# Moving layer-norm and division steps between chunks of a fused attention and feed-forward kernel, and summing its last three chunks tile by tile

## The chip, the core and the metric

The kernel runs on one core of a Trainium2 chip. The metric is device time in microseconds (us). The core has five engines with a queue each: TensorE (PE in the profile; its weight loads are PEld), VectorE (DVE), ScalarE (ACT), GpSimd (POOL) and SyncE (SP), which here only issues transfers (DMAs). Every queue runs in order: an instruction that waits holds up all behind it on its engine. [...]

## What is computed

One transformer block with adaptive layer norm over 2048 tokens of width 512. Cut to what matters:

```python
x = x + ga * attention(layernorm(x) * (1 + ca) + sa)      # 32 heads of 16
h = layernorm(x) * (1 + cb) + sb
x = x + gb * (gelu(h @ w1 + b1) @ w2 + b2)                # 512 -> 1792 -> 512
```

The attention output is divided by the sum of the softmax and multiplied by `wo`. Inputs and outputs are float32.

## The kernel before

Tokens are handled in four blocks of 512 (`NB`, `TB`), which the change's description calls first to fourth; in the code they are 0 to 3. A product of two float32 operands is made from three matmuls on a high and a low part of each operand, so each operand that meets TensorE is first split: a cast gives the high part, a subtraction the low part.

The kernel has three stages: projections, attention, feed-forward. The change touches the last one alone, the loop at lines 984 to 996. It takes 56 steps (`NI`), one for each block and each 128 columns of the 1792 hidden ones; step i is chunk i % 14 of block i // 14. A step does this, in the order in which each engine's queue receives it:

- `load_f(i + 4)`, line 717: SyncE issues the two weight loads of the step four ahead (w1r, w2r, 256 KB each).
- `split_f(i + 2)`, line 724: the weights of the step two ahead are split. VectorE casts w1h (line 728) and w2h (line 730); GpSimd subtracts for w1l (line 729) and w2l (line 731).
- `ffn1(i)`, line 895: 12 matmuls (line 300) into one PSUM bank of the ring `sc`; ScalarE makes g, the gelu (line 903), and ghi (line 906); VectorE subtracts for glo (line 907).
- `ffn2([i - 1])`, line 912: 12 matmuls (line 924) add the step before to four accumulators, one for each tile of 128 tokens: ghi with w2h, ghi with w2l, glo with w2h. So TensorE asks for glo of step i at the third matmul of `ffn2([i])`, which stands in step i + 1. With the last chunk of a block in its list, `ffn2` also ends the block: y = accumulator * gb on VectorE (line 929, four times, three buffers), then x2 + y (line 933) on GpSimd, in the last block on VectorE, and a store from SyncE (line 934). For blocks 0 to 2 that falls into steps 14, 28 and 42.
- the functions that `plan` lists for the step.

The plan carries what the later blocks need. `o_load` (line 758) fetches the attention output of a block as o_b; `o_den` (line 751) inverts the softmax sums and stores them. `o_norm` (line 766) is the division, for each of four parts k: a load of the inverse sums, rb (line 775, SyncE, 256 KB), then on VectorE a multiplication (line 778), a cast (line 779) and a subtraction (line 780). `o_proj` (line 790) is 12 matmuls with `wo` and one addition on VectorE (line 802). `ln2` (line 806) is the layer norm: statistics of four tiles (line 236), a factor rs that GpSimd raises to a power (line 241), and for each tile a pair of VectorE operations, xn_b (line 813) and x2 + b2 (line 814). `ln2_t` (line 819) transposes on TensorE (line 257), lets ScalarE scale into a tile h (line 262) and VectorE split it (lines 263, 264).

`put_ln2` (line 956) spreads a layer norm around a step n that it is given: statistics of three tiles in step n - 1, the fourth and rs in n, two pairs in n + 1, two pairs in n + 2, transposes in n + 4 and n + 5. Nothing is reordered: the four lists are written out by hand in lines 971 to 983.

The buffers that the steps meet: rb and h share three buffers (tag `h32` of `epool`), ghi and glo have three each (lines 904, 905), the split weights four.

Of the kernel before, what the change touches and what calls it, by code (L numbers as in the profile page):

```python
# [22 lines left out]
NF = FF // P  # L23
# [29 lines left out]
def block_kernel(ctx: ExitStack, tc: tile.TileContext, x, wqkv, wo, w1, b1, w2, b2, c, w_mod, out):  # L53
# [4 lines left out]
    def pool(name, bufs=1, **kw):  # L58
        cm = tc.tile_pool(name=name, bufs=bufs, **kw)
        return cm, cm.__enter__()  # L60

    def close(cm):
        cm.__exit__(None, None, None)
# [15 lines left out]
    def bank_mx():  # L79
        return ring("mx")  # L80

    def bank():
        return ring("sc")

    def bank_pv():
        return ring("pv")
# [568 lines left out]
    epool = ctx.enter_context(tc.tile_pool(name="epool", bufs=1, side="right"))  # L655
# [60 lines left out]
    def load_f(i):  # L716
        f = i % NF
        a = fpool.tile([P, KC, P], F32, tag="w1r", name="w1r", bufs=3)
        b = fpool.tile([P, D], F32, tag="w2r", name="w2r", bufs=3)
        sy.dma_start(a, w1[:, f * P : (f + 1) * P].rearrange("(k p) n -> p k n", p=P))  # L720
        sy.dma_start(b, w2[f * P : (f + 1) * P, :])
        raw1[i] = a, b

    def split_f(i):
        a, b = raw1.pop(i)
        ahi, alo = [fpool.tile([P, KC, P], FR, tag=n, name=n, bufs=4) for n in ("w1h", "w1l")]
        bhi, blo = [fpool.tile([P, D], FR, tag=n, name=n, bufs=4) for n in ("w2h", "w2l")]
        ve.tensor_copy(ahi, a)  # L728
        gp.tensor_tensor(alo, a, ahi.bitcast(F32), op=ALU.subtract)  # L729
        ve.tensor_copy(bhi, b)  # L730
        gp.tensor_tensor(blo, b, bhi.bitcast(F32), op=ALU.subtract)  # L731
        wf[i] = ahi, alo, bhi, blo
# [5 lines left out]
    def parts8(pl):  # L738
        if pl is epool:
            t = kts[len(p8) % 2 - 1]  # L740
            p8.append([t[:, i].rearrange("p (k t) -> p k t", k=KC) for i in range(2)])
            return p8[-1]
        return [pl.tile([P, KC, TB], FR, tag=n, name=n, bufs=1) for n in ("h2hi", "h2lo")]
# [7 lines left out]
    def o_den(qb):  # L751
        dn = dns[qb]
        ve.reciprocal(dn, dn)
        sy.dma_start(rden_d[qb].rearrange("h (a f) -> (h a) f", f=P), dn)
# [3 lines left out]
    def o_load(qb):  # L758
        obs[qb] = o_b
        sy.dma_start(obs[qb], o_d[qb].rearrange("(k p) t -> p k t", p=P))  # L760
        if qb < 3:
            oo[qb] = parts8(epool)
        else:
            oo[qb] = [fpool.tile([P, KC, TB], FR, name=f"o3{i}", bufs=1) for i in range(2)]

    def o_norm(qb, k):

        ob = obs[qb]
        ohi, olo = oo[qb]
        eng = ve if qb > 1 else gp  # L770

        def load():
            rbs[qb, k] = epool.tile([P, TB], F32, tag="h32", name="rb", bufs=3)
            r = rden_d[qb][k * 8 : (k + 1) * 8]
            sy.dma_start(rbs[qb, k], bass.AP(tensor=r.tensor, offset=r.offset, ap=[[TB, 8], [0, DH], [1, TB]]))

        return [load,
                lambda: eng.tensor_tensor(ob[:, k], ob[:, k], rbs[qb, k], op=ALU.mult),
                lambda: eng.tensor_copy(ohi[:, k], ob[:, k]),
                lambda: eng.tensor_tensor(olo[:, k], ob[:, k], ohi[:, k].bitcast(F32), op=ALU.subtract)]  # L780
# [3 lines left out]
    def load_x2(qb, x2t):  # L784
        x2[qb] = x2t
        for i in range(4):
            r0 = qb * TB + i * P
            sy.dma_start(x2t[i], x[r0 : r0 + P, :])

    def o_proj(qb, t):  # L790

        ohi, olo = oo[qb]
        ps = []
        sl = slice(t * P, (t + 1) * P)
        terms = [(p[:, i, sl], w[:, i]) for i in range(KC) for p, w in ((ohi, wo_hi), (ohi, wo_lo), (olo, wo_hi))]

        def mm(i):
            if i == 0:
                ps.append(bank() if qb else bank_mx())
            te.matmul(ps[0], *terms[i], start=i == 0, stop=i == len(terms) - 1)  # L800
            if i == len(terms) - 1:
                ve.tensor_tensor(x2[qb][t], ps[0], x2[qb][t], op=ALU.add)

        return [lambda i=i: mm(i) for i in range(len(terms))]

    def ln2(qb):

        mv = small.tile([P, 4, 2], F32, tag="mv", name="mv")
        rs = small.tile([P, 4], F32, tag="rs", name="rs")
        xns[qb] = [xn_b[:, t] for t in range(4)]  # L810

        def rows(t):
            ve.tensor_scalar(xns[qb][t], x2[qb][t], mv[:, t, 0:1], rs[:, t : t + 1], op0=ALU.subtract, op1=ALU.mult)
            ve.tensor_tensor(x2[qb][t], x2[qb][t], b2_b, op=ALU.add)

        return ([lambda t=t: ln_stat(mv, t, x2[qb][t]) for t in range(4)] + [lambda: ln_factor(mv, rs)]
                + [lambda t=t: rows(t) for t in range(4)])

    def ln2_t(qb, pl):
        hi, lo = parts8(pl)  # L820
        tr, evac = transposed(xns.pop(qb), hi, lo, 1, epool, lambda fc: bank(), (ve, ve))
        h2[qb] = hi, lo
        return [lambda fc=fc: evac(fc, tr(fc)) for fc in range(KC)]
# [67 lines left out]
    fcm, fpool = pool("fpool", bufs=2)  # L891
# [20 lines left out]
    def ffn2(fs):  # L912
        qb = fs[0] // NF
        if fs[0] % NF == 0:
            acc[qb] = [bank_mx(), bank_mx(), bank_mx(), bank_pv()]
        ops = []
        for i in fs:
            ghi, glo = gt.pop(i)
            _, _, bhi, blo = wf.pop(i)
            ops += [(i % NF, n, p, q) for n, (p, q) in enumerate(((ghi, bhi), (ghi, blo), (glo, bhi)))]  # L920
        for t in range(4):
            sl = slice(t * P, (t + 1) * P)
            for f, n, p, q in ops:
                te.matmul(acc[qb][t], p[:, sl], q, start=f == 0 and n == 0, stop=f == NF - 1 and n == 2)  # L924
            if ops[-1][0] == NF - 1 and t:
                ts = (0, 1) if t == 1 else (t,)
                ys = [fpool.tile([P, D], F32, tag="y", name="y", bufs=3) for _ in ts]
                for i, y in zip(ts, ys):
                    ve.tensor_tensor(y, acc[qb][i], gb_b, op=ALU.mult)
                for i, y in zip(ts, ys):  # L930
                    r0 = qb * TB + i * P
                    eng = ve if qb == NB - 1 else gp
                    eng.tensor_tensor(x2[qb][i], x2[qb][i], y, op=ALU.add)
                    sy.dma_start(out[r0 : r0 + P, :], x2[qb][i])

    NI = NB * NF
# [16 lines left out]
    def put(qb, f, *fs):  # L953
        plan.setdefault((qb, f), []).extend(fs)

    def put_ln2(qb, at, pl):

        i0 = at[0] * NF + at[1]

        def step(key, make, i):  # L960
            if i == 0:
                steps[key] = make()
            steps[key][i]()

        for i in range(9):
            n = i0 + (-1 if i < 3 else 0 if i < 5 else 1 if i < 7 else 2)
            put(*divmod(n, NF), lambda i=i: step((qb, "l"), lambda: ln2(qb), i))
        for i in range(4):
            put(*divmod(i0 + 4 + i // 2, NF), lambda i=i: step((qb, "t"), lambda: ln2_t(qb, pl), i))

    put(0, 0, lambda: o_load(2), lambda: o_den0(3))
    put(0, 3, lambda: o_den(3))
    put(0, 7, lambda: o_load(3))
    for t in range(4):
        for i, d in enumerate((0, 1, 1, 2)):
            put(0, 1 + t + d, lambda t=t, i=i: o_norm(2, t)[i]())
            put(0, 8 + t + d, lambda t=t, i=i: o_norm(3, t)[i]())
        put(0, 8 + t, lambda t=t: [f() for f in o_proj(2, t)])
        put(1, 5 + t, lambda t=t: [f() for f in o_proj(3, t)])
    put(1, 1, lambda: load_x2(3, x2[0]))  # L980
    put_ln2(1, (0, 1), fpool)
    put_ln2(2, (0, 13), epool)
    put_ln2(3, (1, 11), fpool)
    for i in range(NI):
        qb, f = divmod(i, NF)
        if i + 4 < NI:
            load_f(i + 4)
        if i + 2 < NI:
            split_f(i + 2)
        ffn1(i)  # L990
        if i and i < NI - 2:
            ffn2([i - 1])
        for fn in plan.get((qb, f), []):
            fn()
    ffn2([NI - 3])
    ffn2([NI - 2, NI - 1])
    close(fcm)
    close(kcm)

# [25 lines left out]
```

## Time and profile before

| what | us |
|---|---|
| median of 3 runs (lowest to highest) | 1766.52 (1766.45 to 1767.83) |
| the profiled execution's own time | 1765.35 |
| its span, first to last instruction | 1763.6 |
| the 56 steps, from the first `ffn1` matmul to the last matmul's end | 1420.4 to 1758.6 |

The span is 1.75 us shorter than the profiled execution's own time, and that is 1.17 us under the median. In the timelines a row gives start, busy time, engine, line, operation, output and inputs, and in brackets the engine's idle time before it with what ended it. Where two operations follow each other without idle time, the distance of their starts is what counts: the busy time of a row reaches a little into the next row.

### The profile page before, as it was taken

How to read it: one execution, taken by the hardware profiler on the slowest of the kernel's cores; microseconds unless marked ns; L12 is line 12 of the kernel's file. 1: busy time of each engine (PE TensorE's matmuls, PEld its weight loads, DVE VectorE, ACT ScalarE, POOL GpSimd, SP SyncE). 2: the span in 40 equal slices, each digit the busy share in tenths (PEclk: the TensorE clock that was granted, in tenths of full speed). 3: DMA queues.
4: the chain of work that ended last, by engine and by line, in shares of the span. 5: the costliest groups of instructions: out<-in, count | busy, mean ns of one | idle time of the engine just before them, and what ended most of it. 6: DMA issues, size and time to landing. Idle time of an engine off the chain costs nothing.

```text
span 1763.6 us, 29164 instructions
## 1 busy us (share of the span) xinstructions
PE 1748.7 (99%) x10554; PEld 901.1 (51%) x10554; DVE 1404.5 (80%) x2553; ACT 1355.8 (77%) x2580; POOL 320.1 (18%) x347
## 2 busy tenths in 40 slices
PE   8999999999999999999999999999999999999998
PEld 6755555344343443343343343343433478788887
DVE  6579999898888888888888888888886286838453
ACT  3478888999999999999999999999999732213222
POOL 3204422010000000000000000000003154636462
PEclk9999999999999999999999999999999999999999
DMA  8767636811500411411410101101013064423341
GB/s 277 250 141 163 151 115 130 130 37 29 87 23 23 82 27 23 74 36 23 74 35 24 38 25 33 38 23 36 23 60 104 22 195 131 126 78 114 102 120 48
DMA packets 124100, 144.17 MB, mean 82 GB/s; under 512 B 38930, under 2 KB 72722, under 8 KB 122004
## 3 DMA queue, kind: packets, MB, share of 16 engines
q1 hardware_dynamic: 120644, 135.55, 30.9%
q10 hardware_dynamic: 3312, 6.76, 1.0%
q8 instruction: 83, 1.36, 0.3%
q14 instruction: 61, 0.50, 0.1%
HBM read 106.37 MB, written 35.87 MB: 81 GB/s over the span
## 4 chain that ended last, share of the span: by engine, by line
PE 93%; DVE 3%; DMA 1%; issue 1%; POOL 1%; SPq 0%; ACT 0%; ACTq 0%; DVEq 0%; POOLq 0%
PE pv L693 29%; PE mx L429 19%; PE sc L300 16%; PE sc L860 13%; PE mx L447 6%; PE mx L924 5%; PE pv L924 2%; PE sc L800 1%; PE mx L800 1%; DMA wmod<-in_w_mod_dram 1%; DVE glo L907 0%; POOL w2l L731 0%; DMA rb<-rden 0%; PE sc L257 0%; DVE mxs L431 0%
## 5 line engine op out<-in xcount | busy, mean ns | idle before, releaser
L861 ACT ACTIVATE p<-sc 128x512 f32<-128x512 f32 x2048 | 1054.8, 615 | 39.4 <-PE sc L860 13.4
L431 DVE TENSOR_REDUCE mxs<-mx 128x1 f32<-128x512 f32 x1472 | 927.5, 684 | 112.9 <-PE sc L860 76.6
L693 PE MATMUL pv<-p,vg 128*32 128x512 f32 x4096 | 546.0, 605 | 0.0
L860 PE MATMUL sc<-qst,kq 50*128 50x512 f32 x1024 | 284.1, 435 | 0.0
L860 PE MATMUL sc<-qst,kt 50*128 50x512 f32 x1024 | 282.3, 431 | 0.0
L429 PE MATMUL mx<-kq,qmx 48*128 48x512 f32 x768 | 262.1, 428 | 0.2
L429 PE MATMUL mx<-kt,qmx 48*128 48x512 f32 x704 | 240.3, 428 | 0.1
L429 PEld LDWEIGHTS mx<-kq,qmx 48*128 48x128 f32 x768 | 122.6, 184 | 228.5 <-DVE mxs L431 209.2
L903 ACT ACTIVATE g<-sc,b_c 128x512 f32<-128x512 f32 x56 | 38.6, 690 | 237.2 <-PE sc L300 233.1
L429 PEld LDWEIGHTS mx<-kt,qmx 48*128 48x128 f32 x704 | 113.3, 184 | 208.8 <-DVE mxs L431 191.1
L458 DVE CUSTOM_DVE_ANT_0 cp<-mx,cp 128x512 f32<-128x512 f32 x288 | 187.2, 688 | 36.3 <-PE mx L447 31.3
L471 POOL CAST m<-mn 128x16 fp32r<-128x16 f32 x32 | 6.3, 197 | 1026.0 <-DVE mn L465 1026.0
L454 ACT ACTIVATE cp<-mx 128x512 f32<-128x512 f32 x288 | 156.3, 597 | 38.8 <-PE mx L447 38.4
L693 PEld LDWEIGHTS pv<-p,vg 128*32 128x32 f32 x4096 | 81.1, 108 | 180.7 <-issue 169.3
L860 PEld LDWEIGHTS sc<-qst,kq 50*128 50x128 f32 x1024 | 125.5, 185 | 32.1 <-ACT p L861 23.6
L907 DVE TENSOR_TENSOR glo<-g,ghi 128x512 fp32r<-128x512 f32 x56 | 60.1, 1073 | 94.8 <-ACT ghi L906 94.8
L860 PEld LDWEIGHTS sc<-qst,kt 50*128 50x128 f32 x1024 | 125.5, 185 | 10.1 <-ACT p L861 3.1
L447 PE MATMUL mx<-kt,qmx 48*128 48x512 f32 x576 | 113.4, 455 | 0.0
L729 POOL TENSOR_TENSOR w1l<-w1r,w1h 128x512 fp32r<-128x512 f32 x56 | 76.8, 1372 | 152.7 <-DVE w1h L728 130.5
L447 PEld LDWEIGHTS mx<-kt,qmx 48*128 48x128 f32 x576 | 58.3, 184 | 56.4 <-issue 33.4
L300 PE MATMUL sc<-hThi,w 128*128 128x512 f32 x256 | 84.0, 436 | 2.2 <-DVE hThi L263 2.2
L731 POOL TENSOR_TENSOR w2l<-w2r,w2h 128x512 fp32r<-128x512 f32 x56 | 81.1, 1448 | 6.6 <-DVE w2h L730 6.2
(158 smaller groups left out, 1671.4 us busy)
## 6 DMA issues: line engine op xcount, KB each, us to landing
w1r<-in_B_w_dram SPq DMA_DIRECT2D x56, 256.0 KB
w2r<-in_B_w_dram SPq DMA_DIRECT2D x56, 256.0 KB
qk<-parts SPq DMA_DIRECT2D x25, 512.0 KB
qmx<-qk SPq DMA_DIRECT2D x192, 64.0 KB
qst<-qk SPq DMA_DIRECT2D x192, 64.0 KB
wmod<-in_w_mod_dram SPq DMA_DIRECT2D x6, 1024.0 KB
kq<-qk SPq DMA_DIRECT2D x24, 256.0 KB
kt<-qk SPq DMA_DIRECT2D x24, 256.0 KB
```

The lines of the kernel that those rows point to most:

```text
L300: te.matmul(ps, p, q, start=i == 0, stop=i == len(terms) - 1)
L429: te.matmul(ps, qmx[u][rows, p, qc * P : (qc + 1) * P], kst[u // NB][rows, p, kr * TB : (kr + 1) * TB], start=True, stop=True)
L431: ve.tensor_reduce(mxs[u][:, p, a, qc, kr : kr + 1], ps, axis=AX.X, op=ALU.max, negate=True)
L447: te.matmul(ps, qmx[u][rows, p, qc * P : (qc + 1) * P], kpm[u // NB][rows, p, t0 : t0 + TB], start=True, stop=True)
L454: ac.activation(vabs[n, a], ps, AF.Abs)
L458: ve.tensor_tensor_reduce(v, ps, v, -0.5, 3.0e38, ALU.add, ALU.min, mxs[u][:, p, a, qc, r : r + 1])
L693: te.matmul(cur_pv[0][32 * j : 32 * (j + 1)], vg[g][:, kc, j * VW : j * VW + 32], pt.pop((s, j)), start=kc == 0, stop=kc == NKC - 1)
L729: gp.tensor_tensor(alo, a, ahi.bitcast(F32), op=ALU.subtract)
L731: gp.tensor_tensor(blo, b, bhi.bitcast(F32), op=ALU.subtract)
L860: te.matmul(ps, k[r0 : r0 + KX, p, kc * P : (kc + 1) * P], q[r0 : r0 + KX, p], start=True, stop=True)
L861: ac.activation(pb, ps, AF.Exp, scale=SCALE)
L924: te.matmul(acc[qb][t], p[:, sl], q, start=f == 0 and n == 0, stop=f == NF - 1 and n == 2)
```

## The change

```diff
-    put(0, 7, lambda: o_load(3))
+    put(0, 9, lambda: o_load(3))
     for t in range(4):
         for i, d in enumerate((0, 1, 1, 2)):
-            put(0, 1 + t + d, lambda t=t, i=i: o_norm(2, t)[i]())
-            put(0, 8 + t + d, lambda t=t, i=i: o_norm(3, t)[i]())
-        put(0, 8 + t, lambda t=t: [f() for f in o_proj(2, t)])
-        put(1, 5 + t, lambda t=t: [f() for f in o_proj(3, t)])
+            put(0, 3 + t + d, lambda t=t, i=i: o_norm(2, t)[i]())
+            put(*divmod(10 + t + d, NF), lambda t=t, i=i: o_norm(3, t)[i]())
+        put(0, 9 + t, lambda t=t: [f() for f in o_proj(2, t)])
+        put(1, 6 + t, lambda t=t: [f() for f in o_proj(3, t)])
     put(1, 1, lambda: load_x2(3, x2[0]))
     put_ln2(1, (0, 1), fpool)
-    put_ln2(2, (0, 13), epool)
-    put_ln2(3, (1, 11), fpool)
+    put_ln2(2, (1, 3), epool)
+    put_ln2(3, (1, 12), fpool)
...
-        if i and i < NI - 2:
+        if i and i < NI - 3:
             ffn2([i - 1])
         for fn in plan.get((qb, f), []):
             fn()
-    ffn2([NI - 3])
-    ffn2([NI - 2, NI - 1])
+    ffn2([NI - 4])
+    ffn2([NI - 3, NI - 2, NI - 1])
```

In steps, with block 2 the third and block 3 the fourth:

| work | steps before | steps after |
|---|---|---|
| division of block 2: rb loads; multiplications and casts; subtractions | 1-4; 2-5; 3-6 | 3-6; 4-7; 5-8 |
| `o_load(3)`; division of block 3, the same three | 7; 8-11; 9-12; 10-13 | 9; 10-13; 11-14; 12-15 |
| `o_proj` of block 2; of block 3 | 8-11; 19-22 | 9-12; 20-23 |
| layer norm of block 2: statistics; pairs; transposes | 12-13; 14-15; 17-18 | 16-17; 18-19; 21-22 |
| layer norm of block 3, the same three | 24-25; 26-27; 29-30 | 25-26; 27-28; 30-31 |
| last `ffn2` call | steps 54 and 55, tile by tile | steps 53, 54 and 55, tile by tile |

The layer norm of block 1 stays (statistics 0-1, pairs 2-3, transposes 5-6), and the inversion `o_den(3)` stays in step 3. No instruction is added or dropped.

## The prediction

> **What bounds the kernel now.** I read the page first, then TensorE's waits inside the feed-forward stage, then the timeline around each of them. The page:
>
> ```profile
> span 1763.6 us, 29164 instructions
> PE 1748.7 (99%) x10554; PEld 901.1 (51%) x10554; DVE 1404.5 (80%) x2553; ACT 1355.8 (77%) x2580; POOL 320.1 (18%) x347
> ```
>
> TensorE is busy for 99% of the span, and no matmul comes or goes. So the change can only win or lose at TensorE's stalls and behind the last matmul. All waits of TensorE from 1407 us on, where the stage is, are one row: the matmuls of `ffn2` wait for glo, VectorE's subtraction.
>
> ```profile
> PE mx L924 <- DVE glo L907: 3.4, 4, 2.3
> ```
>
> One of the four is in step 1, where nothing changes; three lie in the changed stretch. The timeline of TensorE has these, in steps 5, 8 and 16, and behind them a fourth, too short to be counted as a wait:
>
> ```profile
> 1448.93 0.39 PE L924 MATMUL mx<-w2l,ghi 128*128 128x512 f32 x1
> 1450.08 0.50 PE L924 MATMUL mx<-w2h,glo 128*128 128x512 f32 x1 [0.76 <-DVE glo L907]
> 1450.41 0.39 PE L924 MATMUL mx<-w2h,ghi 128*128 128x512 f32 x1
> 1450.64 0.39 PE L924 MATMUL mx<-w2l,ghi 128*128 128x512 f32 x1
> ...
> 1468.11 0.39 PE L924 MATMUL mx<-w2l,ghi 128*128 128x512 f32 x1
> 1468.67 0.50 PE L924 MATMUL mx<-w2h,glo 128*128 128x512 f32 x1 [0.17 <-DVE glo L907]
> ```
>
> ```profile
> 1523.38 0.39 PE L924 MATMUL mx<-w2l,ghi 128*128 128x512 f32 x1
> 1526.03 0.50 PE L924 MATMUL mx<-w2h,glo 128*128 128x512 f32 x1 [2.25 <-DVE glo L907]
> ...
> 1531.37 0.39 PE L924 MATMUL mx<-w2l,ghi 128*128 128x512 f32 x1
> 1531.74 0.50 PE L924 MATMUL mx<-w2h,glo 128*128 128x512 f32 x1
> ```
>
> Undisturbed, starts are 0.23 us apart (1450.41 to 1450.64). What exceeds that is the stall; the start behind it comes 0.1 us late too (1450.08 to 1450.41). With that 0.1 each: 1.15 - 0.23 + 0.1 = **1.02** for glo of step 4, 0.56 - 0.23 + 0.1 = **0.43** for step 7, 2.65 - 0.23 + 0.1 = **2.52** for step 15, 0.37 - 0.23 + 0.1 = **0.24** for step 16. That is 4.2 us, 0.24% of the span: all that better placing can win on TensorE.
>
> **Divisions of block 2, two steps later.** VectorE before:
>
> ```profile
> 1435.56 0.80 DVE L778 TENSOR_TENSOR o_b<-o_b,rb 128x512 f32<-128x512 f32 x1 [0.90 <-DMA rb<-rden]
> ...
> 1442.45 0.94 DVE L753 RECIPROCAL dn<-dn 128x128 f32<-128x128 f32 x1
> ...
> 1447.57 0.42 DVE L728 CAST w1h<-w1r 128x512 fp32r<-128x512 f32 x1
> ...
> 1448.24 1.78 DVE L907 TENSOR_TENSOR glo<-g,ghi 128x512 fp32r<-128x512 f32 x1
> ```
>
> It waited 0.90 us for the first rb and then worked through. Ahead of glo of step 4 stood two multiplications with their casts and a subtraction: 1.6 us for the multiplications alone, plus the 0.90. All of it goes behind that glo, which was late by 0.92. The 1.02 goes. For glo of step 7 two subtractions (up to 1.7 each, as glo, which is one), a multiplication and a cast, about 4.4 us, move behind it; it was late by 0.33. The 0.43 goes, unless VectorE stands still for a new reason.
>
> That reason could be rb. The first load of it now goes out in step 3, on SyncE behind the store of the inverted sums, which waits for VectorE's inversion. One landing of rb is named in the chain, and the groups of VectorE give the layer norm's two operations where nothing is beside them:
>
> ```profile
> 1428.77 6.77 DMA rb<-rden
> ```
>
> ```profile
> L814 DVE TENSOR_TENSOR x2a<-x2a,b_b 128x512 f32<-128x512 f32 x8 | 5.5, 692 | 0.3
> L813 DVE TENSOR_SCALAR xn_b<-x2a,mv,rs 128x512 f32<-128x512 f32 x8 | 4.3, 539 | 0.0
> ```
>
> Two pairs take 2 x (0.69 + 0.54) = 2.4 us alone. The inversion ended at 1443.4. Without the 0.90 of idle time, and with contention beside it as before, I put its end at 1442.2, and rb's issue at 1442.7. By the row rb lands 6.8 us later, at 1449.5; that load had a 1 MB load just ahead of it, which this one hasn't. VectorE asks for it behind two layer-norm pairs (2.4), splits (0.7, from 1447.57 to 1448.24) and glo (1.7), at 1447.0: up to 2.5 us of idle time. glo of step 7 ended at 1468.6; less 0.9 and 4.4 it would end at 1463.3. VectorE then outruns ScalarE in steps 5 to 7 and waits for ghi, so I put it at 1465.8; TensorE asks at 1468.11 + 0.23 - 1.02 = 1467.3. That leaves 1.5 us of slack, and a stall between 0 and 1.0. I take 0, for want of the 1 MB. The fourth load has to wait for a buffer that the third multiplication frees; it is in time unless it takes over 6.6 us. Sum of this part: **-1.45**, bounds -1.45 and -0.45.
>
> **Layer norm of block 2, steps 12-18 to 16-22; divisions of block 3.** Around step 14:
>
> ```profile
> 1513.86 0.69 DVE L907 TENSOR_TENSOR glo<-g,ghi 128x512 fp32r<-128x512 f32 x1 [0.36 <-ACT ghi L906]
> 1516.93 5.69 POOL L933 TENSOR_TENSOR x2a<-x2a,y 128x512 f32<-128x512 f32 x4
> 1518.25 0.69 DVE L929 TENSOR_TENSOR y<-pv,gb_b 128x512 f32<-128x512 f32 x1 [1.89 <-POOL x2a L933]
> 1518.86 0.90 DVE L813 TENSOR_SCALAR xn_b<-x2b,mv,rs 128x512 f32<-128x512 f32 x1
> ...
> 1523.54 0.42 DVE L728 CAST w1h<-w1r 128x512 fp32r<-128x512 f32 x1
> ```
>
> The fourth y waits 1.89 us for the first of GpSimd's additions, which begin late behind rs and two splits, and the pairs then take 1523.54 - 1518.86 = 4.68 us beside the additions. Splits and glo need another 1526.03 - 1523.54 = 2.49 us until TensorE goes on. After the change rs and both pairs are gone from here; in their place stand a subtraction, a multiplication and a cast. glo of step 14 only waits for ScalarE, so it comes at 1513.86 - 1.45 = 1512.4; y from 1513.0; the first addition, with no rs ahead of it, from 1513.7 to about 1515.0; the fourth y until 1515.6. The three operations cost 4.3 us if they take turns with the additions as the pairs did, 2.4 us if not (three of the multiplication's 0.8). I take the first, as it is the nearer row: 1519.9, plus 2.49 is 1522.4. TensorE asks at 1523.38 + 0.23 - 1.45 = 1522.2. So 0.2 + 0.1 = **0.3** of the 2.52 stays, bounds 0 and 0.9; the 0.24 of step 16 goes, as only one subtraction stands ahead of its glo. The pairs in steps 18 and 19 (2.4) with splits and glo (2.49) fit into a step of 24 x 0.23 = 5.4 us. The transposes now share steps 21 and 22 with `o_proj`; each bank and each h is used again only a step later, so nothing is charged. Sum: **-2.5**, bounds -2.8 and -1.9.
>
> **Layer norm of block 3, one step later.** Its last two pairs used to run in step 27; now they stand in step 28, behind the four y that end block 1. That is the meeting just taken away from step 14. Before, there:
>
> ```profile
> 1607.98 5.42 POOL L933 TENSOR_TENSOR x2a<-x2a,y 128x512 f32<-128x512 f32 x4
> 1609.31 0.69 DVE L929 TENSOR_TENSOR y<-pv,gb_b 128x512 f32<-128x512 f32 x1 [0.65 <-POOL x2a L933]
> 1609.92 0.90 DVE L728 CAST w1h<-w1r 128x512 fp32r<-128x512 f32 x1
> 1612.47 1.03 PE L257 MATMUL sc<-ident,xn_b 128*128 128x128 f32 x8
> 1613.58 0.39 PE L300 MATMUL sc<-kt,w1l 128*128 128x512 f32 x1
> 1616.55 0.39 PE L924 MATMUL mx<-w2h,glo 128*128 128x512 f32 x1
> ```
>
> In this trace's times VectorE is through with y at 1609.92; two pairs beside the additions add 4.68, splits and glo 2.49: 1617.1. TensorE asked for glo of step 29 at 1616.55, but the eight transposes ahead of it go one step later too (1613.58 - 1612.47 - 0.23 = 0.9), so it asks at 1615.7. A new stall of 1.4 + 0.1 = **1.5**. Below, it is nothing: with pairs of 2.4 us glo is there at 1614.8. Above, it is what step 14 cost, 2.52 + 0.24 = 2.8. I take 1.5, since it comes from the same operations in the same company.
>
> [...]
>
> **The last three chunks.** Each tile of the last call now takes 9 matmuls for 6; TensorE ends at the same place. The end before:
>
> ```profile
> 1758.21 0.39 PE L924 MATMUL pv<-w2h,glo 128*128 128x512 f32 x1
> 1759.06 0.68 DVE L929 TENSOR_TENSOR y<-pv,gb_b 128x512 f32<-128x512 f32 x1
> 1759.78 0.69 DVE L933 TENSOR_TENSOR x2a<-x2a,y 128x512 f32<-128x512 f32 x1
> ```
>
> The last y started 0.46 us after the last matmul's modelled end (1758.60), held up by the tiles before. At 9 x 0.23 = 2.1 us a tile, against y and an addition of 1.4, VectorE keeps up, and the last y starts at 1758.6: **-0.4**, bounds -0.5 and 0. What it may cost: four chunks' ghi and glo now live in three buffers, so ghi of step 55 waits for `ffn2([52])`. From there ScalarE (about 0.6) and VectorE (0.7) take 1.4 us, and TensorE has six matmuls (1.4) before it asks for ghi and eight (1.8) before glo. ghi is covered by 0.8 us, glo by 0.4; I charge nothing.
>
> **Sum.** -1.45 - 2.5 + 1.5 - 0.4 = **-2.8 us** (rounded): the span 1763.6 becomes 1760.8, the profiled execution's 1765.35 becomes 1762.5. That execution is 1.17 us under the median of the runs, so I predict 1766.5 - 2.8 = **1763.7**. About 0.2%, 3.5 us, is what a measurement of this kernel can tell from no change; -2.8 is inside it.
>
> **The rivals.**
> 1. *The stall in step 29 doesn't come*: the pairs get in ahead of the additions. The sum is -4.3, 1762.2, faster. For it: in step 28 y waits 0.65 us, not 1.89. Against: the additions still have 4 us to run when the pairs start.
> 2. *The divisions stay too tight*: contention in steps 4 to 8 leaves VectorE as far behind as now, and that part wins nothing: -1.3, 1765.2. Against: 4.4 us move behind glo of step 7.
> 3. *Slower: rb becomes a wait of its own.* In step 4 and, through the shared buffer, in step 7 VectorE stands idle for rb, with the splits and glo of the next step queued behind, and TensorE waits for these. At a landing of L the first wait is L - 4.3 and the fourth load's L - 6.6; the slack takes 1.5. At 7.5 us the stall is 2.6 and the gain is gone; at 10 us it is 7.6 and the time 1771.3. Against: 6.8 us is the one landing shown, and it had a 1 MB load ahead.
> 4. *It doesn't do what it says*: waits of other causes take the places of those removed, and the time stays at 1766.5.
>
> **How the numbers follow.** Forecast 0.45, rival 1 0.27, rival 2 0.14, rival 4 0.06, rival 3 0.08. Faster by over 0.2% is rival 1 and a little of the forecast's good side (0.30); slower by over 0.2% is rival 3 (0.08); the rest is within 0.2% (0.62). From all bounds at their good end, -4.7, to the forecast's at their bad end (-0.45 - 1.9 + 2.8 = 0.4 more), it would be 1761.8 to 1766.9. The range drops the least likely corner above and gives the run's own spread a little below: 1761.6 to 1766.6.
>
> **What would show it.** The stalls at glo of steps 4, 7 and 16 gone; 0 to 0.9 us left at step 15; a new wait of TensorE for glo at step 29, of 1 to 2 us, with xn_b and x2 + b2 stretched beside GpSimd's additions; no idle time of VectorE for rb, or under 2.5 us; the last y straight behind the last matmul. A wait for ghi at the end, or TensorE waiting for glo in steps 5 to 8, would prove me wrong.

## The result and the profile after

The changed kernel takes 1764.01 us (median of 20 runs, 1762.43 to 1766.63), the kernel before 1767.01 us in the same session (20 runs, 1766.2 to 1769.26). The medians differ by 3.0 us. The ratio of the runs is 0.9981, with a 95% interval of 0.9974 to 0.9987: 0.19% less, a small gain that is clear of no change. The profiled execution of the changed kernel took 1764.5 us. Its page:

```profile
span 1762.7 us, 29158 instructions
PE 1748.9 (99%) x10554; PEld 901.7 (51%) x10554; DVE 1404.5 (80%) x2553; ACT 1356.1 (77%) x2580; POOL 321.1 (18%) x347
```

The amount of work is the same on every engine. The spans differ by only 0.9 us, and that number misleads: in this execution the last stage began 1.6 us later (1422.04 for 1420.43), which this change has no part in. The measure for a change in the last stage is the stage itself: from the first matmul of `ffn1` to the end of the last addition. The first matmul in the timeline of TensorE, before and after, then VectorE's last two operations after:

```profile
1420.43 0.40 PE L300 MATMUL sc<-kt,w1h 128*128 128x512 f32 x1
```

```profile
1422.04 0.40 PE L300 MATMUL sc<-kt,w1h 128*128 128x512 f32 x1
...
1758.20 0.69 DVE L929 TENSOR_TENSOR y<-pv,gb_b 128x512 f32<-128x512 f32 x1 [0.62 <-PE pv L924]
1758.93 0.69 DVE L933 TENSOR_TENSOR x2a<-x2a,y 128x512 f32<-128x512 f32 x1
```

Before, the last addition ended at 1759.78 + 0.69 = 1760.47, so the stage took 340.04 us. After, it takes 1758.93 + 0.69 - 1422.04 = 337.58 us: **-2.46 us**. Below, "the stage" is this length, taken in the same way from each trace.

TensorE's waits from 1407 us on (in all, how often, the longest) are down from 3.4 us to this row, of which 0.2 us is the unchanged wait in step 1:

```profile
PE mx L924 <- DVE glo L907: 1.7, 2, 1.5
```

The timeline of TensorE after, at glo of steps 15 and 29:

```profile
1523.42 0.39 PE L924 MATMUL mx<-w2l,ghi 128*128 128x512 f32 x1
1523.93 0.50 PE L924 MATMUL mx<-w2h,glo 128*128 128x512 f32 x1
...
1613.10 0.39 PE L924 MATMUL mx<-w2l,ghi 128*128 128x512 f32 x1
1615.03 0.50 PE L924 MATMUL mx<-w2h,glo 128*128 128x512 f32 x1 [1.54 <-DVE glo L907]
```

With the prediction's reckoning (0.23 us is the normal distance, 0.1 us for the late start behind it): 0.51 - 0.23 + 0.1 = 0.4 us is left at step 15, and 1.93 - 0.23 + 0.1 = 1.8 us is new at step 29. Nothing is left at steps 4, 7 and 16. VectorE behind its fourth y, in the two meetings with GpSimd, sets these two numbers. First step 14 (division of block 3 behind the y), then step 28 (two layer-norm pairs behind the y):

```profile
1516.60 0.69 DVE L929 TENSOR_TENSOR y<-pv,gb_b 128x512 f32<-128x512 f32 x1 [0.21 <-POOL x2a L933]
1517.21 1.16 DVE L780 TENSOR_TENSOR o<-o_b,o 128x512 fp32r<-128x512 f32 x1
1518.30 1.78 DVE L778 TENSOR_TENSOR o_b<-o_b,rb 128x512 f32<-128x512 f32 x1
1520.11 1.40 DVE L779 CAST o<-o_b 128x512 fp32r<-128x512 f32 x1
1521.43 0.41 DVE L728 CAST w1h<-w1r 128x512 fp32r<-128x512 f32 x1
```

```profile
1607.25 0.69 DVE L929 TENSOR_TENSOR y<-pv,gb_b 128x512 f32<-128x512 f32 x1 [0.21 <-POOL x2a L933]
1607.86 0.90 DVE L813 TENSOR_SCALAR xn_b<-x2a,mv,rs 128x512 f32<-128x512 f32 x1
1608.79 1.67 DVE L814 TENSOR_TENSOR x2a<-x2a,b_b 128x512 f32<-128x512 f32 x1
1610.38 1.52 DVE L813 TENSOR_SCALAR xn_b<-x2a,mv,rs 128x512 f32<-128x512 f32 x1
1611.93 0.69 DVE L814 TENSOR_TENSOR x2a<-x2a,b_b 128x512 f32<-128x512 f32 x1
1612.54 0.42 DVE L728 CAST w1h<-w1r 128x512 fp32r<-128x512 f32 x1
```

And GpSimd beside the second, its four additions in one row:

```profile
1605.91 5.70 POOL L933 TENSOR_TENSOR x2a<-x2a,y 128x512 f32<-128x512 f32 x4 [1.23 <-DVE y L929]
```

What counts are the widths. The same operation, x2 + b2 (L814), takes 1.67 us while GpSimd adds (until 1611.61) and 0.69 us right behind it. The two pairs take 1612.54 - 1607.86 = 4.68 us.

### The profile page after: what moved, and what is told of

The parts are those of the page before. It is cut to its first block, busy times and chain, and to the rows that moved or that the text cites. A ratio compares the mean times of both kernels' runs of the same rounds, so it can differ in the third digit from the quotient of the medians.

```text
span 1762.7 us, 29158 instructions
## 1 busy us (share of the span) xinstructions
PE 1748.9 (99%) x10554; PEld 901.7 (51%) x10554; DVE 1404.5 (80%) x2553; ACT 1356.1 (77%) x2580; POOL 321.1 (18%) x347
## 4 chain that ended last, share of the span: by engine, by line
PE 96%; DVE 2%; DMA 0%; issue 0%; ACT 0%; POOL 0%; SPq 0%; ACTq 0%; DVEq 0%
PE pv L693 29%; PE mx L429 20%; PE sc L300 17%; PE sc L860 13%; PE mx L924 6%; PE mx L447 6%; PE pv L924 2%; PE sc L800 2%; PE mx L800 1%; PE sc L257 1%; DMA wmod<-in_w_mod_dram 0%; DVE glo L907 0%; PE mx L257 0%; PE sc L203 0%; DVE mxs L431 0%
```

## The experiments

**Theory A** is the prediction's: four parts, each worth its stall, and the stall at a block's end comes from VectorE's operations taking turns with GpSimd's additions. **Theory B** is, in each experiment, the rival that would explain the same trace otherwise: VectorE is simply full there, the company doesn't matter, or the parts count alone as they count together.

The table gives each kernel's runs against the kernel before, and its stage against 340.04 us. The runs of one kernel spread by about 0.2%, while the stage differs by 0.03 us between two traces of the kernel before (last section), so single parts are read from the stage. The traces of `e2_div` and `e5_ln3` hold a stretch in which TensorE ran at half its rate (starts 0.43 us apart in place of 0.23); their text says how much of the stage that is.

| kernel | median us | ratio to before, 95% interval | stage against before |
|---|---|---|---|
| the change | 1764.01 | 0.9981 (0.9974 to 0.9987) | -2.46 |
| `e1_ln3_back` | 1762.89 | 0.9979 (0.9969 to 0.9989) | -4.36 |
| `e2_div` | 1769.01 | 1.0012 (1.0003 to 1.0021) | +2.61 |
| `e3_ln2` | 1764.87 | 0.9985 (0.9977 to 0.9994) | -2.84 |
| `e4_tail` | 1767.28 | 1.0001 (0.9992 to 1.0009) | -0.47 |
| `e5_ln3` | 1769.35 | 1.0013 (1.0005 to 1.0022) | +3.12 |
| `e6_best` | 1760.67 | 0.9965 (0.9951 to 0.9979) | -4.79 |
| `e7_addve` | 1763.27 | 0.9981 (0.9972 to 0.9990) | -2.46 |
| `e8_ln3_13` | 1763.95 | 0.9987 (0.9978 to 0.9996) | -2.78 |
| `e9_noadd` | 1762.07 | 0.9972 (0.9960 to 0.9983) | -4.32 |
| `e10_order` | 1763.85 | 0.9984 (0.9975 to 0.9993) | -3.25 |

### The change without its third part

```diff
-    put_ln2(3, (1, 12), fpool)
+    put_ln2(3, (1, 11), fpool)
```

> The changed kernel with the layer norm of block 3 put back to where it was (its pairs in steps 26 and 27). Theory A (the two pairs behind the four y of block 1 take turns with GpSimd's additions and make glo of step 29 late): the stall of 1.8 us at step 29 goes, every other stall stays, so 1.8 us less than the changed kernel, 4.3 to 4.9 us less than the kernel before (about 0.27%). Theory B (VectorE is late at step 29 for another reason, such as the whole stretch being full): the stall stays at 1 us or more and the time is that of the changed kernel, 3.0 us less than before.

The stage is 1.9 us shorter than the changed kernel's, and TensorE's waits in it are one row:

```profile
PE mx L924 <- DVE glo L907: 0.2, 1, 0.2
```

That is step 1. Theory A holds: the stall at step 29 belongs to this edit alone, and the change would have been worth 4.4 us without it.

### The divisions alone

The kernel before with the `o_load`, `o_norm` and `o_proj` lines of the change, and nothing else.

> The kernel before with the division edits alone (both blocks' divisions, the fourth load and the projections later), layer norms and end as before. Theory A: the stalls of steps 4 and 7 go (-1.45), but the layer norm of block 2 is still at steps 12 to 18, so that behind the four y of block 0 there now stand two pairs and the division of block 3: the stall of step 15 grows from 2.5 to about 4.5, that of step 16 from 0.2 to 1.7 or more; in all 2 us slower than before. Theory B (the parts simply add up, each worth the same alone as together): -1.45 us, with step 15 still at 2.5.

The stalls of steps 4 and 7 are gone here too, but the stage is 2.61 us longer. VectorE and then TensorE around step 15:

```profile
1517.78 1.16 DVE L780 TENSOR_TENSOR o<-o_b,o 128x512 fp32r<-128x512 f32 x1
...
1522.01 0.53 DVE L813 TENSOR_SCALAR xn_b<-x2b,mv,rs 128x512 f32<-128x512 f32 x1
```

```profile
1522.01 0.39 PE L924 MATMUL mx<-w2l,ghi 128*128 128x512 f32 x1
1526.85 0.79 PE L924 MATMUL mx<-w2h,glo 128*128 128x512 f32 x1 [4.45 <-DVE glo L907]
1527.44 0.63 PE L924 MATMUL mx<-w2h,ghi 128*128 128x512 f32 x1
```

Division and layer norm now stand one behind the other, after the y: 4.84 - 0.23 = 4.6 us of stall where 2.5 was. Theory B falls, as step 15 didn't stay at 2.5: the 1.45 us that these edits win at steps 4 and 7 is lost again at step 15 while the layer norm stays where it was. The size came out near the 2 us expected, but not by the way expected. There is no stall at step 16, where 1.7 was expected; instead the matmuls behind the stall start 0.43 us apart in place of 0.23, over eleven distances from 1526.85 to 1531.70 (the first is 0.59), which costs 4.85 - 11 x 0.227 = 2.4 us (last section). So nearly all of the 2.61 us is this slow stretch; the stalls alone come out within 0.5 us of the kernel before.

### The layer norm of block 2 alone

The kernel before with `put_ln2(2, (1, 3), epool)` alone.

> The kernel before with the layer norm of block 2 moved alone, the divisions where they were. Theory A: the stalls of steps 15 and 16 (2.5 and 0.2) go down to 0 to 0.4, as the pairs no longer meet GpSimd's additions; those of steps 4 and 7 stay at 1.0 and 0.4: -2.4 to -2.8 us against before. Theory B (this stretch is full whatever stands in it): the stall comes back elsewhere in steps 15 to 20 and the gain is under 1 us.

The stage is 2.84 us shorter, and only the stalls of the first two steps and of steps 4 and 7 remain. Theory A holds, at its upper end: at step 15 nothing is left here. So the 0.4 us left there by the whole change is the division of block 3, not something in the stretch itself.

### The last three chunks alone

The kernel before with the edits of the loop's end alone.

> The kernel before with the last three chunks summed tile by tile alone. Theory A: the last y starts right behind the last matmul, -0.4 us against before, with no wait of TensorE at the end. Theory B: ghi of step 55, which waits for a buffer, holds TensorE up, 0 to +1 us against before.

The stage is 0.47 us shorter and TensorE waits nowhere at the end. Theory A, in the trace; the runs (0.9992 to 1.0009) can't tell it from nothing.

### The layer norm of block 3 alone

The kernel before with `put_ln2(3, (1, 12), fpool)` alone.

> The kernel before with the layer norm of block 3 one step later alone. Theory A: the stall at glo of step 29 comes as in the changed kernel (1.8 us), and those of steps 4, 7, 15 and 16 stay: +1.8 us against before. Theory B (the stall at 29 comes from VectorE running late from the other edits): no stall at 29, within 0.3 us of before.

The stall comes, 1.94 - 0.23 + 0.1 = 1.8 us by the starts on TensorE, so theory A holds on its cause. The stage is 3.12 us longer, 1.3 more than that: in this execution too the matmuls behind the stall of step 15, which this kernel shares with the kernel before, ran at half the rate for a time. That cost 1.6 us (last section) and hid the 0.24 of step 16.

### Without the additions, or with them on VectorE

The changed kernel with GpSimd's four additions of block 1 left out (that part of the output is then missing), and with the same additions on VectorE:

```diff
+                    if qb != 1:
                         eng.tensor_tensor(x2[qb][i], x2[qb][i], y, op=ALU.add)
```

```diff
-                    eng = ve if qb == NB - 1 else gp
+                    eng = ve if qb in (1, NB - 1) else gp
```

> The changed kernel without the four additions that end block 1 (that part of the output is left out), so that VectorE's queue in step 28 is the same but GpSimd has nothing to do beside the two pairs. Theory A (turns with GpSimd's additions): the pairs take 2.4 us in place of 4.7, glo of step 29 is in time, the stall of 1.8 us goes to 0 and the time to 1.8 us under the changed kernel. Theory B (the length of VectorE's queue alone): the pairs stay near 4.7 us and the stall at 1.8.

> The changed kernel with the four additions that end block 1 on VectorE in place of GpSimd, so that the two pairs of step 28 have no GpSimd operation beside them, while VectorE's queue gets longer by four additions (4 x 0.6 us). Theory A (the pairs are stretched from 2.4 to 4.7 us by the additions beside them): the pairs shrink back to 2.4 us, which pays for the additions, and the stall at 29 stays at 1.8 us, within 0.5. Theory B (only the length of VectorE's queue decides, the company does not matter): the stall grows by 2.4, to 4.2 us, and the time by 2.4 us.

VectorE in step 28, first without the additions, then with them in its own queue:

```profile
1607.77 0.53 DVE L813 TENSOR_SCALAR xn_b<-x2a,mv,rs 128x512 f32<-128x512 f32 x1
1608.34 0.69 DVE L814 TENSOR_TENSOR x2a<-x2a,b_b 128x512 f32<-128x512 f32 x1
1608.95 0.54 DVE L813 TENSOR_SCALAR xn_b<-x2a,mv,rs 128x512 f32<-128x512 f32 x1
1609.52 0.69 DVE L814 TENSOR_TENSOR x2a<-x2a,b_b 128x512 f32<-128x512 f32 x1
1610.13 0.42 DVE L728 CAST w1h<-w1r 128x512 fp32r<-128x512 f32 x1
```

```profile
1609.48 0.54 DVE L813 TENSOR_SCALAR xn_b<-x2a,mv,rs 128x512 f32<-128x512 f32 x1
...
1611.24 0.69 DVE L814 TENSOR_TENSOR x2a<-x2a,b_b 128x512 f32<-128x512 f32 x1
1611.85 0.42 DVE L728 CAST w1h<-w1r 128x512 fp32r<-128x512 f32 x1
```

In both the pairs take 2.36 to 2.37 us (1610.13 - 1607.77 and 1611.85 - 1609.48), where they took 4.68 beside GpSimd. Without the additions the stall is gone and the stage 1.86 us shorter than the changed kernel's. With the additions on VectorE the 2.3 us saved on the pairs pays for four additions of 0.6, and the stage is that of the changed kernel to 0.01 us. This shows directly that the additions stretch the pairs, and it shows the price: in this step GpSimd's four additions weren't free for VectorE, they cost it as much time as doing them itself.

### The pairs ahead of the y

The changed kernel with the planned functions of step 28 run ahead of `ffn2([27])`; the instructions are the same, only VectorE's order changes:

```diff
+        late = plan.get((qb, f), [])
+        if i == 2 * NF:
+            for fn in late:
+                fn()
+            late = []
         if i and i < NI - 3:
             ffn2([i - 1])
-        for fn in plan.get((qb, f), []):
+        for fn in late:
             fn()
```

> The changed kernel with one reordering: in step 28 VectorE's two pairs stand ahead of the four y instead of behind them; every instruction is the same. Theory A (what counts is that the pairs come while GpSimd adds): the pairs take 2.4 us in place of 4.7, as the additions haven't begun, and the wait for glo of step 29 goes; but the four y come 2.4 us later and hold their banks, so TensorE waits 0.9 us for the first y and about 0.5 for the fourth: 1.4 us of stall in place of 1.8, 0.2 to 0.8 us less than the changed kernel. Theory B (the amount of work between two glo decides, wherever it stands): pairs and y are the same work, glo of step 29 stays 1.8 us late.

```profile
1604.48 0.53 DVE L813 TENSOR_SCALAR xn_b<-x2a,mv,rs 128x512 f32<-128x512 f32 x1
...
1606.23 0.69 DVE L814 TENSOR_TENSOR x2a<-x2a,b_b 128x512 f32<-128x512 f32 x1
1606.84 1.88 DVE L929 TENSOR_TENSOR y<-mx,gb_b 128x512 f32<-128x512 f32 x3
```

The pairs take 2.36 us, and the stage is 0.79 us shorter than the changed kernel's, at the good end of what theory A expected. The stall for glo of step 29 is gone; TensorE now waits 0.92 us at the first matmul of `ffn2([28])`, and not again for the fourth y, which was expected at 0.5. The expected cause, the bank that the first y still reads, isn't shown: TensorE started at 1607.67, the first of the three y ended at about 1607.5, and ScalarE's g, which the trace names and which the matmul doesn't read, ended at 1607.64.

### One more step later

```diff
-    put_ln2(3, (1, 12), fpool)
+    put_ln2(3, (1, 13), fpool)
```

> The changed kernel with the layer norm of block 3 one more step later, so that block 1 ends exactly as block 0 did in the kernel before: rs just ahead of the splits, the first two pairs behind the four y, the other two one step on. Theory A: the meeting costs what it cost there, 2.5 us at glo of step 29 and 0.2 at step 30 in place of 1.8: about 1 us more than the changed kernel. Theory B (only the two pairs behind the y count, and they stand there already): the stall stays at 1.8 and the time within 0.3 us of the changed kernel.

Both theories missed. The stall at step 29 went down to 1.3 us, with 0.2 at step 30, and the stage is 0.3 us shorter than the changed kernel's. The pairs behind the y take 4.68 us as before, but all four y come earlier. Just ahead of the y stands glo of step 28. In the changed kernel two pairs of step 27 stand ahead of the casts of step 28, so GpSimd's subtractions come late and glo meets the second of them; here no pairs stand there, and glo comes 0.7 us into it. GpSimd's subtraction and that glo in the changed kernel, and the glo here:

```profile
1603.39 1.29 POOL L731 TENSOR_TENSOR w2l<-w2r,w2h 128x512 fp32r<-128x512 f32 x1
```

```profile
1603.58 1.66 DVE L907 TENSOR_TENSOR glo<-g,ghi 128x512 fp32r<-128x512 f32 x1 [1.29 <-ACT ghi L906]
```

```profile
1601.84 1.11 DVE L907 TENSOR_TENSOR glo<-g,ghi 128x512 fp32r<-128x512 f32 x1 [2.48 <-ACT ghi L906]
```

glo, which alone takes 0.69 us, starts 0.19 us behind the start of GpSimd's operation in the changed kernel and ends 0.56 us behind its end, as if it had waited for it; here it ends 0.55 us behind the end of the same operation. Why glo takes longer beside it isn't shown. The 0.55 us by which the two glo differ fits the difference of the two stalls at step 29 (1.81 and 1.28). So the 1.89 us that y waited in step 14 of the kernel before didn't come from the layer norm's place alone; which of the other work around it made it wait stays open.

### A version that beats both

The changed kernel without its third part, and the divisions of block 3 one step earlier:

```diff
-            put(*divmod(10 + t + d, NF), lambda t=t, i=i: o_norm(3, t)[i]())
+            put(*divmod(9 + t + d, NF), lambda t=t, i=i: o_norm(3, t)[i]())
...
-    put_ln2(3, (1, 12), fpool)
+    put_ln2(3, (1, 11), fpool)
```

> The changed kernel with the layer norm of block 3 put back and the divisions of block 3 one step earlier than the change puts them (first multiplication in step 9), so that less of them stands behind the four y of block 0. Theory A: the stalls of steps 4, 7, 16 and 29 are gone, and that of step 15 goes down from 0.4 to 0 to 0.2: 2.0 to 2.2 us less than the changed kernel, 4.7 to 5.3 less than before. Theory B (the operations of the division cost the same wherever they stand in this stretch): the stall comes back in steps 10 to 14, and the time is that of the changed kernel less 1.8.

Theory A holds: the stall of step 15 is gone as well, the stage is 4.79 us shorter than before and 2.33 shorter than after (2.0 to 2.2 was expected), and the ratio to before is 0.9965 (0.9951 to 0.9979). From step 2 on TensorE waits for nothing in this stage. What is left of it, about 1 us in the first two steps, was not touched by any of these edits.

## Why the prediction was right

The forecast was -2.8 us, 1763.7; the runs gave -3.0 and 1764.01, the stage -2.46. That the two times lie within 0.3 us is in part luck: the forecast starts from 1766.5, the median of 3 runs, and the 20 runs beside the change gave 1767.01. The runs' gain is 0.5 us more than the stage's; their interval, 2.3 to 4.6 us, holds both, and what the rest is stays open. The prediction also took 3.5 us for the least that runs can tell from no change; with 20 runs of each kernel, 3.0 was clear. By its steps:

- **Divisions of block 2, -1.45.** Measured: both stalls gone, -1.45, and with them the second rival. The open point was rb. SyncE's issue, behind the store of the inverted sums, and VectorE after:

```profile
1443.85 0.33 SPq L754 DMA_DIRECT2D rden<-dn  x1
1444.27 0.60 SPq L775 DMA_DIRECT2D rb<-rden  x1
```

```profile
1442.88 0.94 DVE L753 RECIPROCAL dn<-dn 128x128 f32<-128x128 f32 x1
...
1446.89 1.78 DVE L907 TENSOR_TENSOR glo<-g,ghi 128x512 fp32r<-128x512 f32 x1
1448.79 1.58 DVE L778 TENSOR_TENSOR o_b<-o_b,rb 128x512 f32<-128x512 f32 x1
```

The store went out 0.03 us behind the end of the inversion (1442.88 + 0.94 = 1443.82), and rb's load 0.42 us behind the store. The multiplication starts 1.90 us behind glo's start; behind two later glo of this trace the next operation starts 1.69 to 1.70 us behind (1458.68 to 1460.37, 1465.93 to 1467.63). So rb landed within 4.5 us of its issue, in time or 0.2 us late, where up to 2.5 us of idle time had been allowed for; the slack covers that, and TensorE didn't wait. The fourth load, issued at 1457.09, had until 1469.33. So the third rival falls, and the choice of 0 was right. That the 6.8 us before came from the 1 MB load ahead is argued, not shown.

- **Layer norm of block 2, -2.5.** Measured: -2.52 - 0.24 + 0.4 = -2.36. The three operations of the division took 1521.43 - 1517.21 = 4.22 us beside the additions, for 4.3 taken; so the choice between 4.3 and 2.4 was right. The closeness is in part luck, as the prediction doesn't show how 4.3 follows from the pairs: their own stretch, 4.68 for 2.4, would have given 4.7.
- **Layer norm of block 3, +1.5.** Measured: +1.8. The pairs took 4.68 us, as taken, and splits and glo 2.49 (1612.54 to 1615.03). The missing 0.3 is the start: I took the moment at which VectorE is through with y from the trace of before. Against the start of the last matmul of its bank that was 1609.92 - 1606.80 = 3.12 us; it is 1607.86 - 1604.48 = 3.38 after. The fourth y waits less (0.21 us for 0.65), but glo of step 28 ahead of it now begins just behind a subtraction of GpSimd and takes 1.66 us, where it took 0.97. The experiments with the additions left out or moved show that the cause was named rightly, and the first rival (no stall) falls. (By the prediction's own rows the additions had 1607.98 + 5.42 - 1609.92 = 3.5 us to run when the pairs would start, not 4; after, it was 1611.61 - 1607.86 = 3.75.)
- **The last three chunks, -0.4.** Measured: -0.43, and -0.47 alone. The last matmul, and ScalarE's ghi of step 55:

```profile
1757.78 0.39 PE L924 MATMUL pv<-w2h,glo 128*128 128x512 f32 x1
```

```profile
1749.88 0.63 ACT L906 ACTIVATE ghi<-g 128x512 fp32r<-128x512 f32 x1 [1.86 <-PE pv L924]
```

The last y starts 1758.20 - 1757.78 = 0.42 us behind the start of that matmul, where it was 1759.06 - 1758.21 = 0.85. The cover for ghi and glo of step 55 held: ghi waited 1.86 us for its buffer, and TensorE waited for neither.

The sum of the measured parts is -1.45 - 2.36 + 1.81 - 0.43 = -2.43, for -2.46 of the stage, and the fourth rival, a time unchanged by waits of other causes, falls too. What the prediction didn't say is that its first two parts hang together: by themselves the divisions lose 2.6 us, 2.4 of it at half rate behind the longer stall.

## What to carry to other kernels

An operation of GpSimd is not free for VectorE just because it runs on another engine: beside its additions two layer-norm pairs took 4.68 us in place of 2.36, as much more as doing the additions on VectorE cost, while y, which reads an accumulator of `ffn2`, kept its 0.69 us beside them. So place VectorE's due work ahead of such a burst (in `e10_order` that took 0.79 us off the changed kernel's stage) or well behind it (in `e3_ln2`, 2.84 us off the stage before). Edits to a schedule that meet in one step don't add up: what one is worth is read with the others in place, so try them by taking one out as well as by putting one in. And measure a change in one stage by that stage's own length in the trace, once the granted clock there has been looked at.

## What the runs showed of the hardware

**Two executions of one kernel differed ahead of the stage, not in it.** The kernel before, profiled once more, took 1769.11 us:

> The kernel before, once more, for its trace: in two of the traces so far (the divisions alone, the last layer norm alone) TensorE's matmuls ran at half the rate for 3 to 5 us right behind the stall at step 15, at a granted clock of 0.5 to 0.67, while the first trace of the kernel before shows full clock behind the same stall of 2.4 us. Theory A (the clock falls behind a long stall in some executions and not in others): either may come here; with half rate the time is 1.5 to 2.4 us above the first trace's stage. Theory B (the kernel decides): full clock behind the stall, as in the first trace.

```profile
1424.22 0.40 PE L300 MATMUL sc<-kt,w1h 128*128 128x512 f32 x1
...
1763.54 0.69 DVE L933 TENSOR_TENSOR x2a<-x2a,y 128x512 f32<-128x512 f32 x1
```

This execution was 3.8 us slower (1769.11 against 1765.35), and reached the stage 1424.22 - 1420.43 = 3.8 us later; its stage took 1763.54 + 0.69 - 1424.22 = 340.01 us, for 340.04 in the first trace. So a difference of tenths of a us in this stage can be read from two traces, as long as neither holds a slow stretch as below; between the runs it is lost in a spread of 4 us.

**Behind the stall of step 15 TensorE ran at half its rate in two of five executions.** These are windows just behind the stall of step 15 (TensorE's busy time and instructions, granted clock, share of the DMA engines, GB/s), for the divisions alone, the last layer norm alone, and the kernel before once more, where the stall ended at 1529.81:

```profile
1525.00:1530.00 5.00, 3.15 (x8) 0.50 0.88 312
```

```profile
1525.00:1530.00 5.00, 4.09 (x11) 0.67 1.00 324
```

```profile
1530.00:1535.00 5.00, 5.00 (x23) 1.00 0.94 297
```

The stall of 4.6 us in the first ends at half the clock. The stall of 2.4 us at step 15 is the same in the second, the third, the first trace of before and the kernel with the last chunks alone; the clock fell in one of these four executions. These kernels differ only from step 24 on, so what they do up to step 15 doesn't decide the fall (theory A, though the repeat itself stayed at full clock, and no single kernel has been seen both ways). In the second the slow stretch ran as follows:

```profile
1526.71 0.61 PE L924 MATMUL mx<-w2h,glo 128*128 128x512 f32 x1
...
1530.11 0.42 PE L300 MATMUL sc<-h2hi,w1l 128*128 128x512 f32 x1
```

From 1526.71 to 1530.11 is 3.4 us with eight distances of 0.43 us, 1.6 us more than at 0.23. In the first it was 4.85 us. The granted clock of whole executions fits a fall in every run of the divisions alone: it was 0.995 or 0.996 in all eleven, and 0.997 or 0.998 in all eleven of the layer norm of block 2 alone, where no such stall is left; but the eight of `e1_ln3_back`, which hasn't got it either, had 0.996 to 0.998. By estimate, 4.85 us at half clock lower the mean of 1766 us by 0.0014. What makes the clock fall, and what ends the slow stretch, isn't shown. A pause of 2.64 or 2.65 us between two starts was followed by half rate in one execution of four. Pauses of 1.68 to 1.94 us were followed by full rate in all three traces that have one (the change, the layer norm of block 3 alone, the additions on VectorE), at a granted clock of 1.00 from 1600 to 1760 us. So where the clock fell, the stall of step 15 cost more than its length, 2.4 us more in the first trace and 1.6 us in the second; in the eight traces in which the layer norm of block 2 stands in steps 16 to 22, the granted clock was 1.00 from 1420 to 1600 us.
